# A retention layer with a gated feed-forward layer on one core: when two units' loads and transposes are issued

## Chip, cores and metric

One core of a Trainium2 chip. The metric is the device time of one execution in microseconds (us). Engine names in the profile: PE is the matrix engine (PEld its weight loads), DVE the vector engine, ACT the scalar engine, POOL is GpSimd, SP is SyncE, which here only issues transfers; a "q" behind a name is that engine's sequencer.

## The reference

A retention recurrence over 768 steps for 4 batches and 8 heads of 64, with one decay per head, then RMS normalisation and a SwiGLU layer over all 3072 tokens:

```
gamma = 1.0 - 2.0 ** (-5.0 - np.arange(H))
for t in range(S):
    state = gamma[None, :, None, None] * state + einsum('bhd,bhe->bhde', k[:, :, t], v[:, :, t])
    y[:, :, t] = scale * einsum('bhd,bhde->bhe', q[:, :, t], state)
x = y.transpose(0, 2, 1, 3).reshape(B * S, H * D)          # 3072 x 512
xn = x / sqrt(mean(x * x) + 1e-6) * rms_g
g = xn @ w_gate                                            # 512 x 1536
out = (g * sigmoid(g) * (xn @ w_val)) @ w_out              # 1536 x 512
```

Inputs and output are float32.

## The kernel before

The 768 steps are cut into six chunks of 128. A chunk has four **units**, one a batch, written (c, b); two units are a **pair** (c, p), and the j-th unit of a pair is (c, p, j). Chunks 0 and 1 use a paired layout of rows; chunks 2 to 5 use plain units.

A unit from chunk 2 on is worked as follows. `load(c, b)` (L105) issues three transfers on POOL's queue: q and k, cast to bf16, and v. `t_dma(c, b)` (L470) issues two transposing transfers on SP's queue, qb to qT and kb to kT. `vp` (L466) scales v by the decay on POOL. `a_pe` (L480) makes the scores on PE, `a_mask` (L489) masks them on DVE. `values(c, p)` (L504) makes for a pair y_ps (scores times v), kv_ps (the update of the state) and y_ps again (q times state); with `then` it makes a pair's scores (`a_pair`, two `a_pe`) at its end. Then come `y_out` (DVE), `state_add` (DVE), `square` (ACT), `rstd` (POOL: m at L454, the power at L370), `state_cast` (POOL, L348), `norm` (DVE, L462) and `x_dma(c, p, j)` (L541), a transposing transfer on SP that fills xnT, the feed-forward layer's input. x(2,1,1) below is such a transfer. In chunk 1 two further helpers, `tp1` and `tc1`, transpose q and k on PE and copy them out as q2T and k2T, `ap` makes the scores (L280), and `x_pe` and `x_copy` transpose xn on PE.

The feed-forward layer of a chunk is a row of `gv` steps (L548: eight g_ps and eight v_ps matmuls of 256 tokens, or four and four of 512, a sigmoid-weighted unit on ACT, a product on DVE into hT) and four `down(c, b)` (L576: twelve matmuls of hT with w_out into o_ps, a copy to o_sb on ACT, a store on SP; o_sb has three buffers). It lags one chunk behind: while PE runs the feed-forward steps of chunk c, the retention work of chunk c+1 and the loads of chunk c+2 are put between the steps.

The order is written out by hand. Every engine and every queue serves its instructions in program order. The first part of the program is a plain list of calls; from chunk 1's feed-forward on, `run(steps, after)` calls the steps and, behind step number i, whatever `after[i]` lists. One dictionary (L752) serves chunk 1's steps: 0 to 5 are `gv` of the first 256 tokens, 6 to 11 of the second, 12 to 15 the downs. Another (L785) serves chunks 2 to 5: steps 0 and 1 are `gv` of the first 256 tokens, 2 and 3 of the second, 4 to 11 `gv` of all 512, 12 to 15 the downs. d there is the chunk in its retention phase and d+1 the one being loaded.

PSUM has eight banks. `bank` hands them out in a fixed rotation up to chunk 1's feed-forward (`split`), and after that four for the feed-forward and four for the retention work.

Of the kernel before, what the change touches and what calls it, by code (L numbers as in the profile page):

```python
# [16 lines left out]
def kernel(  # L17
# [21 lines left out]
    NFF = DFF // 128  # L39
# [25 lines left out]
    def bank(name, dtype=F32, ffn=False, i=None):  # L65
        if i is None and split[0]:
            i = turn[ffn] % 4 + 4 * ffn
            turn[ffn] += 1
        elif i is None and first:
            i = first.pop(0)  # L70
        elif i is None:
            i = order[0]
            order.append(order.pop(0))
        return psum.tile([128, 512 if dtype == F32 else 1024], dtype, name=name, tag=f"p{i}")
# [30 lines left out]
    def load(c, b, names="qkv"):  # L105
        u = U.setdefault((c, b), {})
        for n in names:
            if n == "v":
                x = work.tile([128, H, D], F32, name="v_f", tag="v_f", bufs=6)
                nc.gpsimd.dma_start(out=x, in_=unit_v[n][c, b])  # L110
            else:
                x = work.tile([128, DM], BF16, name=n + "b", bufs=8)
                nc.gpsimd.dma_start(out=x.rearrange("p (h d) -> p h d", h=H), in_=unit_v[n][c, b])  # L113
            u[n] = x
# [106 lines left out]
    def copy(eng, out, in_):  # L221
        return (nc.scalar.copy if eng == "a" else nc.vector.tensor_copy)(out, in_)  # L222
# [44 lines left out]
    def ap(c, p, a):  # L267
        u = U[c, p]
        if c == 0:
            qt, kt = ([u[n + "T", a][:, :, b] for b in range(2)] for n in "qk")  # L270
        else:
            qt, kt = u["qT", a], u["kT", a]
        ps = [bank("a_ps") for _ in range(2)]
        for x in range(2):
            for e in range(2):
                o = (x * 2 + e) * 128
                for b in range(2):
                    for i in range(2):
                        r, t = slice(i * 64, i * 64 + 64), slice(b * 64, b * 64 + 64)
                        nc.tensor.matmul(ps[i][t, o:o + 128], kt[b][r, x, e], qt[b][r, x], start=True, stop=True)  # L280
        u["a_ps", a] = ps
# [104 lines left out]
    def x_pe(c, p, j):  # L386
        u = U[c, p]
        ps = bank("x_ps", BF16)
        for s in range(KS):
            nc.tensor.transpose(ps[:, s * 128:(s + 1) * 128], u["xn"][j][:, s * 128:(s + 1) * 128], ident)  # L390
        u["x_ps", j] = ps

    def x_copy(c, p, j, eng):
        b = 2 * p + j
        dst = XT[c][:, :, b * C:(b + 1) * C]
        src = U[c, p]["x_ps", j][:, :512].rearrange("p (s t) -> p s t", s=KS)
        if c == 0 and j == 0:
            nc.vector.tensor_tensor(out=dst, in0=src, in1=g_col[:, :, None].to_broadcast([128, KS, 128]), op=ALU.mult)
        else:
            return copy(eng, dst, src)  # L400
# [71 lines left out]
    def t_dma(c, b):  # L472
        u = U[c, b]
        for n in "qk":
            t = work.tile([128, NHP, 128], BF16, name=n + "T", tag=n + "T", bufs=8)
            nc.sync.dma_start_transpose(out=t, in_=u[n])
            u[n + "T"] = t
# [91 lines left out]
    def store(eng, c, b, m, o_sb):  # L569
        if c < 2:  # L570
            for e in range(2):
                eng.dma_start(out=out_e[c, b, e][:, m], in_=o_sb[e * 64:e * 64 + 64, m])
        else:
            eng.dma_start(out=out_v[c, b][:, m], in_=o_sb[:, m])

    def down(c, b):  # L576
        ps = bank("o_ps", ffn=True)
        for n in range(NFF):
            nc.tensor.matmul(ps, HT[c][:, n, b * C:(b + 1) * C], wo_b[:, n, :], start=n == 0, stop=n == NFF - 1)  # L579
        o_sb = work.tile([128, DM], F32, name="o_sb", bufs=3)  # L580
        nc.scalar.copy(o_sb, ps)  # L581
        store(nc.sync, c, b, slice(0, DM), o_sb)
# [125 lines left out]
    load(2, 0)  # L708
    y1(0)
    down(0, 0)  # L710
    y1_out(0)
    square(1, 0, 0)
# [5 lines left out]
    vp_pair(1, 1)  # L718
    load(2, 2)
    down(0, 1)  # L720
    down(0, 2)
    t_dma(2, 0)
    for n, e in (("q", "a"), ("k", "v")):
        tp1(1, n)
        tc1(1, n, e)
# [1 line left out]
    x_copy(1, 0, 0, "v")  # L727
    x_pe(1, 0, 1)
    x_copy(1, 0, 1, "v")
    ap(1, 1, 0)  # L730
    ap(1, 1, 1)
    for a in range(2):
# [1 line left out]
            ap_mask(1, 1, a, i)  # L734
    load(2, 3)
    t_dma(2, 1)
    down(0, 3)

    def run(steps, after):
        for i, step in enumerate(steps):  # L740
            step()
            for f in after.get(i, ()):
                f()

    def L(f, *a):
        return lambda: f(*a)
# [13 lines left out]
        5: [L(a_pair, 2, 0), L(a_mask, 2, 0, 0)],  # L760
        6: [L(a_mask, 2, 0, 1), L(a_mask, 2, 1, 0), L(vp, 2, 2), L(vp, 2, 3)],
        7: [L(a_mask, 2, 1, 1)],
        8: [L(values, 2, 0), L(y_out, 2, 0, 0), L(y_out, 2, 0, 1), L(state_add, 2, 0), L(load, 3, 2),
            L(t_dma, 3, 0), L(t_dma, 3, 1)],
        9: [L(square, 2, 0, 0), L(load, 3, 3)],
        10: [L(a_pair, 2, 1), L(square, 2, 0, 1), L(a_mask, 2, 2, 0), L(a_mask, 2, 2, 1), L(state_cast, 0),
             L(rstd, 2, 0)],
        11: [L(a_mask, 2, 3, 0), L(a_mask, 2, 3, 1), L(t_dma, 3, 2)],
        12: [L(values, 2, 1, (3, 0), True), L(norm, 2, 0, 0, 1), L(x_dma, 2, 0, 0), L(x_dma, 2, 0, 1),
             L(y_out, 2, 1, 0), L(y_out, 2, 1, 1), L(square, 2, 1, 0), L(square, 2, 1, 1), L(rstd, 2, 1),  # L770
             L(state_add, 2, 1), L(a_mask, 3, 0, 0), L(a_mask, 3, 0, 1), L(norm, 2, 1, 0, 1),
             L(x_dma, 2, 1, 0), L(x_dma, 2, 1, 1), L(t_dma, 3, 3), L(a_mask, 3, 1, 0, 1),
# [3 lines left out]
    for c in range(2, NCH):  # L776

        steps = [L(gv, c, n, n + 2, t, t + 256) for t in (0, 256) for n in (0, 2)]
        steps += [L(gv, c, n, n + 1, 0, GT) for n in range(4, NFF)]
        steps += [L(down_last if (c, b) == (NCH - 1, B - 1) else down, c, b) for b in range(B)]  # L780
        d = c + 1
        more = d + 1 < NCH
        after = {}
        if d < NCH:
            after = {  # L785
                0: [L(begin, d)] + [L(load, d + 1, 0)] * more,
                1: [L(values, d, 0)] + [L(load, d + 1, 1)] * more,
                2: [L(y_out, d, 0, 0), L(vp, d, 2), L(vp, d, 3)],
                3: [L(y_out, d, 0, 1)] + [L(state_add, d, 0)] * more,
                4: [L(square, d, 0, 0)] + [L(t_dma, d + 1, 0)] * more,  # L790
                5: [L(a_pair, d, 1), L(a_mask, d, 2, 0), L(square, d, 0, 1), L(rstd, d, 0)]
                   + [L(state_cast, 0), L(t_dma, d + 1, 1)] * more,
                6: [L(a_mask, d, 2, 1), L(norm, d, 0, 0), L(x_dma, d, 0, 0)] + [L(load, d + 1, 2)] * more,
                7: [L(norm, d, 0, 1), L(x_dma, d, 0, 1), L(a_mask, d, 3, 0)] + [L(vp, d + 1, 0)] * more,
                8: [L(a_mask, d, 3, 1)] + [L(load, d + 1, 3), L(vp, d + 1, 1)] * more,
            }
            if more:
                after.update({
                    11: [L(values, d, 1, (d + 1, 0), True), L(y_out, d, 1, 0), L(y_out, d, 1, 1),
                         L(square, d, 1, 0), L(square, d, 1, 1), L(rstd, d, 1), L(state_add, d, 1),  # L800
                         L(a_mask, d + 1, 0, 0), L(a_mask, d + 1, 0, 1), L(norm, d, 1, 0, 1), L(x_dma, d, 1, 0)],
                    12: [L(x_dma, d, 1, 1), L(a_mask, d + 1, 1, 0, 1), L(state_cast, 1), L(t_dma, d + 1, 2)],
                    13: [L(t_dma, d + 1, 3)],
                })
            else:
                after.update({
                    9: [L(values, d, 1)],
                    10: [L(y_out, d, 1, 0)],
                    11: [L(y_out, d, 1, 1), L(square, d, 1, 0), L(square, d, 1, 1), L(rstd, d, 1)],
                    12: [L(norm, d, 1, 0, 1), L(x_dma, d, 1, 0), L(x_dma, d, 1, 1)],  # L810
                })
        run(steps, after)
# [28 lines left out]
```

## Time and profile before

| | us |
|---|---|
| median of 4 runs | 239.37 (238.26, 238.68, 240.06, 242.51) |
| the profiled execution | 237.91 |
| its span, first to last instruction | 236.1 |
| PE busy in it | 225.9 |

The granted PE clock is full throughout. The busy tenths of PE and of the transfer engines over 40 equal slices of 5.9 us:

```
PE   7986999999999999998999999999999999999994
DMA  7999999999999999899993999992530204200022
```

In the list of issues the q and k loads of a unit take a median of 6.0 and 6.7 us from issue to landing, v 7.1; the transposes qT 6.4, kT 7.7 and xnT 4.2.

To read the views: a row of the timeline gives start, duration, engine, line, operation and tiles, the number of instructions merged into it, and in brackets the engine's idle time before it with what ended that. A row of the waits gives who waited for whom: total us, times, longest. A row of the chain gives start, duration, and what held the chain then. A queue's row gives packets, MB, and the packets' time as a share of 16 engines.

### The profile page before, as it was taken

Reading aid. Unit: us, or ns where it says so; the run is one execution under the profiler, and the core shown is the slowest. Engines: PE = TensorE matmul, PEld = TensorE weight load, DVE = VectorE, ACT = ScalarE, POOL = GpSimd, SP = SyncE. Lnnn points to the kernel's source line nnn. Section 1 sums busy time; section 2 is a strip of 40 time slices with the busy share of each in tenths; the row PEclk is TensorE's granted clock in tenths of the full one; section 3 lists DMA queues with packets and bytes.
Section 4 is the critical chain, followed back from the end, with each engine's and each line's share of the span. In section 5 each row is a group of like instructions: output and inputs, shape, how many; then the busy total and the mean of one; then the engine's idle time right before and its main releaser. Section 6 shows DMA issues by size and latency. Waiting matters only on the chain.

```text
span 236.1 us, 5540 instructions
## 1 busy us (share of the span) xinstructions
PE 225.9 (96%) x2268; PEld 138.6 (59%) x2290; DVE 127.4 (54%) x222; ACT 87.5 (37%) x176; POOL 114.9 (49%) x150
## 2 busy tenths in 40 slices
PE   7986999999999998999999999999999999999994
PEld 2445785545898864684454684454774544854443
DVE  3675743828396787346967046967155742244300
ACT  2865535242343433225323235332325241333211
POOL 8967699759689934952927703917001000000000
PEclk9999999999999999999999999999999999999999
DMA  7999999999999999899993999992530204200022
GB/s 99 162 191 204 180 166 181 198 200 227 155 147 196 157 156 210 89 212 194 106 122 25 177 165 214 112 113 70 136 109 0 47 0 144 81 0 0 0 92 90
DMA packets 83307, 30.25 MB, mean 128 GB/s; under 512 B 69521, under 2 KB 78993, under 8 KB 83282
## 3 DMA queue, kind: packets, MB, share of 16 engines
q0 software_dynamic: 51328, 16.52, 72.5%
q1 hardware_dynamic: 31280, 13.25, 29.2%
q8 instruction: 18, 0.29, 0.5%
q10 hardware_dynamic: 674, 0.14, 0.3%
q14 instruction: 7, 0.06, 0.1%
HBM read 28.32 MB, written 6.29 MB: 147 GB/s over the span
## 4 chain that ended last, share of the span: by engine, by line
PE 83%; DMA 8%; POOL 4%; DVE 2%; issue 1%; ACT 1%; POOLq 0%; DVEq 0%
PE v_ps L560 25%; PE g_ps L560 24%; PE o_ps L579 24%; DMA wv_b<-in_moe_w_val_dram 4%; DMA kT<-kb 4%; PE a_ps L485 1%; PE y_ps L514 1%; POOL q2b L101 1%; POOL k2b L101 1%; PE o_ps L590 1%; PE y_ps L531 1%; PE kv_ps L523 1%; POOL wg_b L86 1%; PE kv_ps L329 1%; DVE x L440 1%
## 5 line engine op out<-in xcount | busy, mean ns | idle before, releaser
L565 DVE TENSOR_TENSOR hT<-sg,v_ps 128x512 bf16<-128x512 bf16 (+1 forms) x76 | 49.9, 658 | 76.0 <-PE v_ps L560 64.6
L560 PE MATMUL v_ps<-xnT,wv_b 128*128 128x256 bf16 (+1 forms) x427 | 74.9, 309 | 1.9 <-DMA wv_b<-in_moe_w_val_dram 1.6
L560 PE MATMUL g_ps<-xnT,wg_b 128*128 128x256 bf16 (+1 forms) x417 | 73.8, 308 | 0.8 <-ACT xnT L222 0.2
L564 ACT ACTIVATE sg<-g_ps 128x512 bf16<-128x512 f32 (+1 forms) x76 | 43.5, 575 | 74.8 <-PE g_ps L560 70.5
L579 PE MATMUL o_ps<-wo_b,hT 128*128 128x512 bf16 x269 | 60.6, 379 | 0.4
L560 PEld LDWEIGHTS <-wv_b 128*128 128x128 bf16 x428 | 41.7, 98 | 22.8 <-DMA wv_b<-in_moe_w_val_dram 2.2
L560 PEld LDWEIGHTS <-wg_b 128*128 128x128 bf16 x428 | 40.5, 98 | 21.1 <-issue 0.7
L579 PEld LDWEIGHTS <-hT 128*128 128x128 bf16 x276 | 26.6, 98 | 31.6
L454 POOL TENSOR_SCALAR m<-ms 128x2 f32<-128x2 f32 x10 | 2.2, 218 | 69.7 <-ACT xsq L449 69.6
L581 ACT COPY o_sb<-o_ps 128x512 f32<-128x512 f32 x23 | 13.5, 585 | 46.1 <-PE o_ps L579 42.5
L462 DVE SCALAR_TENSOR_TENSOR xn<-x,rstd,g_bc 128x512 bf16<-128x512 f32 x20 | 19.5, 1005 | 9.3 <-POOL rstd L370 9.3
L494 DVE TENSOR_TENSOR am<-a_ps,causal 128x512 bf16<-128x512 f32 x32 | 21.1, 681 | 0.0
L468 POOL TENSOR_TENSOR vp<-v_f,vd_n 128x512 bf16<-128x512 f32 x16 | 19.4, 1236 | 0.0
L449 ACT ACTIVATE xsq<-x 128x512 bf16<-128x512 f32 x20 | 12.4, 623 | 9.3 <-DVE x L440 9.3
L113 POOL DMA_DIRECT2D kb<-in_k_dram x16 | 14.4, 898 | 1.9 <-DMA wo_b<-in_moe_w_out_dram 1.9
L113 POOL DMA_DIRECT2D qb<-in_q_dram x16 | 15.1, 943 | 0.0
L110 POOL DMA_DIRECT2D v_f<-in_v_dram x16 | 14.7, 921 | 0.0
L440 DVE TENSOR_TENSOR x<-y_ps,yd_n 128x512 f32<-128x512 f32 x16 | 10.6, 685 | 1.7 <-PE y_ps L531 1.7
L219 PE MATMUL hot<-ones 128*128 128x512 bf16 x25 | 9.6, 503 | 1.5 <-DVE ones L146 1.4
L300 POOL TENSOR_TENSOR vp<-v2f,vd_p 128x1024 bf16<-128x1024 f32 x4 | 7.7, 1928 | 0.4 <-DMA v2f<-in_v_dram 0.4
L370 POOL TENSOR_TENSOR rstd<-m,mhalf 128x2 f32<-128x2 f32 x10 | 7.2, 718 | 0.8
L101 POOL DMA_DIRECT2D q2b<-in_q_dram x8 | 5.8, 736 | 0.8 <-POOLq L825 0.8
(96 smaller groups left out, 154.7 us busy)
## 6 DMA issues: line engine op xcount, KB each, us to landing
v_f<-in_v_dram POOLq DMA_DIRECT2D x16, 256.0 KB, 7.1
out_dram<-o_sb SPq DMA_DIRECT2D x15, 256.0 KB, 2.3
out_dram<-o_sb SPq DMA_DIRECT2D x17, 128.0 KB, 5.5
qb<-in_q_dram POOLq DMA_DIRECT2D x16, 128.0 KB, 6.0
kb<-in_k_dram POOLq DMA_DIRECT2D x16, 128.0 KB, 6.7
wg_b<-in_moe_w_gate_dram POOLq DMA_DIRECT2D x6, 256.0 KB, 7.9
wv_b<-in_moe_w_val_dram POOLq DMA_DIRECT2D x6, 256.0 KB, 8.6
wo_b<-in_moe_w_out_dram POOLq DMA_DIRECT2D x3, 512.0 KB, 8.9
```

What stands on the lines that cost most here:

```text
L110: nc.gpsimd.dma_start(out=x, in_=unit_v[n][c, b])
L113: nc.gpsimd.dma_start(out=x.rearrange("p (h d) -> p h d", h=H), in_=unit_v[n][c, b])
L440: nc.vector.tensor_tensor(out=x[:, :, :, i, :], in0=u["y"][i].rearrange("p (b a d) -> p b a d", b=2, a=NHP), in1=yd_n[:, c, i][:, None, :, ...
L449: nc.scalar.activation(xsq, u["x"][:, b], AF.Square, scale=1.0 / math.sqrt(DM), accum_out=u["ms_"][:, b:b + 1])
L462: nc.vector.scalar_tensor_tensor(out=u["xn"][b], in0=u["x"][:, b], scalar=u["rstd"][:, b:b + 1], in1=g_bc, op0=ALU.mult, op1=ALU.mult)
L468: nc.gpsimd.tensor_tensor(out=x, in0=U[c, b]["v"], in1=vd_n[:, c, :, None].to_broadcast([128, H, D]), op=ALU.mult)
L494: nc.vector.tensor_tensor(out=x, in0=u["a_ps"][i].rearrange("p (a t) -> p a t", a=NHP), in1=causal[:, None, :].to_broadcast([128, NHP, 128 ...
L560: nc.tensor.matmul(x[:, o:o + w], wt[:, s, n * 128:(n + 1) * 128], XT[c][:, s, t0:t1], start=s == 0, stop=s == KS - 1)
L564: nc.scalar.activation(sg[:, :m], ps[0][:, :m], AF.Silu)
L565: return nc.vector.tensor_tensor(out=HT[c][:, n0:n1, t0:t1], in0=sg[:, :m].rearrange("p (n t) -> p n t", t=w), in1=ps[1][:, :m].rearrange( ...
L579: nc.tensor.matmul(ps, HT[c][:, n, b * C:(b + 1) * C], wo_b[:, n, :], start=n == 0, stop=n == NFF - 1)
L581: nc.scalar.copy(o_sb, ps)
```

## The change

`down` can be given a part of its twelve matmuls: n0 to n1 into the same bank, with copy and store behind the last part alone. Otherwise instructions only change places:

- Chunk 0's feed-forward: the two transposes of unit (2,0) go before `down(0, 2)` instead of behind it; `down(0, 3)` is cut into four matmuls ahead of `ap(1, 1, 0)` and eight at its old place.
- Chunk 1's steps: `load(3, 2)` from step 8 to 11, `load(3, 3)` from step 9 to 12; the transposes of (3,2) from step 11 into step 12, between the x transposes of the pairs (2,0) and (2,1). Those of (3,3) stay behind the latter.
- Chunks 2 and 3 (d+1 is 4 and 5): `load(d+1, 0)` and `load(d+1, 1)` from steps 0 and 1 to 1 and 3, the transposes of these units from steps 4 and 5 to 5 and 6, and `load(d+1, 2)` to the head of step 6's list.

```diff
-    def down(c, b):
-        ps = bank("o_ps", ffn=True)
-        for n in range(NFF):
+    DP = {}
+
+    def down(c, b, n0=0, n1=NFF):
+        ps = DP[b] = bank("o_ps", ffn=True) if n0 == 0 else DP[b]
+        for n in range(n0, n1):
             nc.tensor.matmul(ps, HT[c][:, n, b * C:(b + 1) * C], wo_b[:, n, :], start=n == 0, stop=n == NFF - 1)
+        if n1 < NFF:
+            return
...
     down(0, 1)
+    t_dma(2, 0)
     down(0, 2)
-    t_dma(2, 0)
...
     x_copy(1, 0, 1, "v")
+    down(0, 3, 0, 4)
     ap(1, 1, 0)
     ap(1, 1, 1)
...
     t_dma(2, 1)
-    down(0, 3)
+    down(0, 3, 4)
...
-        8: [L(values, 2, 0), L(y_out, 2, 0, 0), L(y_out, 2, 0, 1), L(state_add, 2, 0), L(load, 3, 2),
+        8: [L(values, 2, 0), L(y_out, 2, 0, 0), L(y_out, 2, 0, 1), L(state_add, 2, 0),
             L(t_dma, 3, 0), L(t_dma, 3, 1)],
-        9: [L(square, 2, 0, 0), L(load, 3, 3)],
+        9: [L(square, 2, 0, 0)],
...
-        11: [L(a_mask, 2, 3, 0), L(a_mask, 2, 3, 1), L(t_dma, 3, 2)],
+        11: [L(a_mask, 2, 3, 0), L(a_mask, 2, 3, 1), L(load, 3, 2)],
         12: [L(values, 2, 1, (3, 0), True), L(norm, 2, 0, 0, 1), L(x_dma, 2, 0, 0), L(x_dma, 2, 0, 1),
+             L(t_dma, 3, 2), L(load, 3, 3),
...
-                0: [L(begin, d)] + [L(load, d + 1, 0)] * more,
-                1: [L(values, d, 0)] + [L(load, d + 1, 1)] * more,
+                0: [L(begin, d)],
+                1: [L(values, d, 0)] + [L(load, d + 1, 0)] * more,
                 2: [L(y_out, d, 0, 0), L(vp, d, 2), L(vp, d, 3)],
-                3: [L(y_out, d, 0, 1)] + [L(state_add, d, 0)] * more,
-                4: [L(square, d, 0, 0)] + [L(t_dma, d + 1, 0)] * more,
+                3: [L(y_out, d, 0, 1)] + [L(state_add, d, 0), L(load, d + 1, 1)] * more,
+                4: [L(square, d, 0, 0)],
                 5: [L(a_pair, d, 1), L(a_mask, d, 2, 0), L(square, d, 0, 1), L(rstd, d, 0)]
-                   + [L(state_cast, 0), L(t_dma, d + 1, 1)] * more,
-                6: [L(a_mask, d, 2, 1), L(norm, d, 0, 0), L(x_dma, d, 0, 0)] + [L(load, d + 1, 2)] * more,
+                   + [L(state_cast, 0), L(t_dma, d + 1, 0)] * more,
+                6: [L(t_dma, d + 1, 1), L(load, d + 1, 2)] * more + [L(a_mask, d, 2, 1), L(norm, d, 0, 0), L(x_dma, d, 0, 0)],
```

## The prediction

> **What bounds the kernel now.** I began with the busy shares on the page, then the matrix engine's own waits from 40 us on, then its timeline around the two it shows, then the chain of waits into the longer one, and last the two queues that feed that chain.
>
> ```profile
> PE 225.9 (96%) x2268; PEld 138.6 (59%) x2290; DVE 127.4 (54%) x222; ACT 87.5 (37%) x176; POOL 114.9 (49%) x150
> ```
>
> ```profile
> PE a_ps L485 <- DMA kT<-kb: 0.8, 1, 0.8
> PE a_ps L280 <- ACT q2T L222: 0.2, 1, 0.2
> ```
>
> PE is busy for 225.9 of 236.1 us, and from 40 us on it waits over 0.15 us only twice. Both waits lie in code that the diff touches. The change adds and removes no arithmetic, so what it can gain is these two waits; what it can lose is any new one.
>
> ```profile
> 55.97 0.24 PE L280 MATMUL a_ps<-q2T,k2T 64*64 64x128 bf16 x2
> 56.41 0.63 PE L280 MATMUL a_ps<-q2T,k2T 64*64 64x128 bf16 x30 [0.19 <-ACT q2T L222]
> ...
> 88.85 0.39 PE L485 MATMUL a_ps<-qT,kT 64*128 64x128 bf16 x8
> 90.06 0.40 PE L485 MATMUL a_ps<-qT,kT 64*128 64x128 bf16 x8 [0.82 <-DMA kT<-kb]
> ```
>
> ```profile
> 81.27 8.75 DMA kT<-kb
> 90.01 0.05 issue
> 90.06 0.40 PE a_ps L485 x8
> ```
>
> The first stall is at `ap(1,1,0)`: PE has the scores' first operand but not the second q2T copy. The second is at `a_pe(3,1)`: its k transpose was issued at 81.27 and landed 8.75 us later. What stood beside that transfer is in the GpSimd and SyncE timelines:
>
> ```profile
> 77.60 0.94 POOL L113 DMA_DIRECT2D qb<-in_q_dram  x1
> 78.52 0.91 POOL L113 DMA_DIRECT2D kb<-in_k_dram  x1
> 79.38 0.93 POOL L110 DMA_DIRECT2D v_f<-in_v_dram  x1
> 80.26 0.93 POOL L113 DMA_DIRECT2D qb<-in_q_dram  x1
> 81.12 0.94 POOL L113 DMA_DIRECT2D kb<-in_k_dram  x1
> 81.99 0.96 POOL L110 DMA_DIRECT2D v_f<-in_v_dram  x1
> ```
>
> ```profile
> 85.01 1.19 SPq L476 DMA_TRANSPOSE qT<-qb  x1
> 86.30 2.09 SPq L476 DMA_TRANSPOSE kT<-kb  x1
> 88.49 1.19 SPq L572 DMA_DIRECT2D out_dram<-o_sb  x2
> 89.77 7.71 SPq L543 DMA_TRANSPOSE xnT<-xn  x4
> ```
>
> The six loads of units (3,2) and (3,3) are issued from 77.60 to 82.95, exactly around the transposes of (3,1) at 79.77 and 81.27. Transposes with little beside them land fast: 2.4 us at the least (x transposes, after 160 us).
>
> **Part 1: the split down and t_dma(2,0).** Four of the twelve matmuls of `down(0,3)` come before `ap(1,1,0)`. In the timeline the twelve run at a pitch of 0.216 us, so four fill 55.97 to 56.84. The awaited q2T copy ended at 56.35, the k2T copies at 56.25: the thirty-two score matmuls then run unbroken. Before, the third of them started at 56.41 although the first two started at 55.97: 0.43 us lost, of which the page calls 0.19 idle (the rest is the pipeline's tail). The split costs one more switch of matmul shapes; the nearest rows are groups after a switch, 0.98 against 0.87 us for the same eight matmuls at 62.88: 0.11. Bounds of the cost: 0 and 0.22 (two switches); I take 0.1. Gain 0.33. The bank order moves with it, o_ps(0,3) taking the bank that a_ps had, and each a_ps the next one: the new owners of the score banks are the copies of `down(0,2)` (ended at 55.38) and of q2T and k2T (56.35), all before 56.84. The first bank of the next stage, for g_ps at about 59.2, was read by the second mask, which ended at 58.11 before and ends about 0.5 later: no wait.
>
> Of `t_dma(2,0)` two transposes pass two stores of `down(0,2)` on SP. They were issued at 56.61 and 58.10 and can go when kb(2,0) is there (landed at 54.93), so SP is free of `t_dma(2,1)` about 2.2 us sooner; that waits for kb(2,1) at 59.34 and so is issued at 59.7 rather than 61.91. Its k took 9.5 us and landed at 71.4, needed at 72.09: a cover of 0.7 us that PE's gain would eat, and that grows to about 2.5. The stores go 2 us later; their o_sb is wanted again at 93.19. Gain of the move itself: nothing.
>
> **Part 2: loads and transposes of (3,2), (3,3).** On POOL the order becomes cast of the state, m, rstd(2,0), then the six loads. The cast waits for the state add (ended at 81.16), m for the last square (83.27, now 0.3 sooner), rstd takes 0.72: the loads run from about 83.9 to 89.4 instead of 77.6 to 82.95. Behind them on POOL stands rstd(2,1), whose square ended at 91.77 and will end near 90.4: a cover of 1.0 us. If it were gone, norm(2,1) and its transposes would slip by the same amount.
>
> So (3,1)'s transposes have no newly issued load beside them from 77.6 on, only the tail of those issued until 75.6 (landed at 82.7). kT(3,1) lands at 81.27 plus 2.4 to 7.5 (the k of (3,0) before it took 7.0, q 7.5), thus 83.7 to 88.8; I take 86. PE asks at 89.07 less 0.33: even the upper bound arrives in time. The weight loads of that line waited 1.0 us and the matmuls started 0.99 us late (last start before 89.02, next 90.06, pitch 0.05). Gain 0.99, of which 0.82 is idle.
>
> What comes next: on SP the order becomes stores of `down(1,0)`, x(2,0,0), x(2,0,1), q and k of (3,2), x(2,1,0), x(2,1,1), then (3,3). With stores at 88.2 and each transpose taking 1.2 to 1.3 us to issue: x(2,0) from 89.5 to 92.1, (3,2) to 94.6 (its q is loaded from 83.9 and lands between 5.3 and 10.2 us later by the rows of that tile, 89.2 to 94.1; nearest is 5.3, of the load that met the emptiest queues), x(2,1,0) to 95.9, x(2,1,1) issued at 95.9. Before, that last one was issued at 95.45 and took 4.4 us. Landing at 100.3. PE wants it at 102.94 less the 1.3 gained, 101.6. No wait, with 1.3 us to spare. (3,3) is issued at the same 97.6 as before, and wanted at 110. Cost taken: 0.
>
> **Part 3: chunk 4, and chunk 5 the same way.** The vp products of the running chunk (2.10 us for two) pass before the second unit's loads on POOL; on SP nothing changes order from `t_dma(4,0)` on. Loads of (4,1), issued from 99.00, move by 2.1 less 1.3: 0.8 later. kT(4,1) is issued at 108.92, wanted at 122.25. For chunk 5: issue at 129.37, scores at 157.09. Cost 0 both times, covered by some ten us. One place is tight already: the last x transpose of chunk 3, issued at 129.20, took 8.3 us and landed at 137.5, wanted at 137.77. It moves with PE, and the loads of (5,1) issued beside it at 129.37 now come 2.1 us after: if anything it gets room.
>
> [...] Transposes without loads beside them took 4.1 and 4.4 us (x(2,1)); with loads beside them 5.0 and 8.3 us (x(3,1)). In the stretch from 86 to 89 us the two queues moved the same number of packets:
>
> ```profile
> q1 hardware_dynamic: 885, 0.22, 96.0%
> q0 software_dynamic: 881, 0.11, 80.5%
> ```
>
> [...]
>
> By the rows, what decides is x(2,1,1). At 8.3 us it would land at 104.2, 2.6 us late, and the sum would be +1.3. At 4.4 it is -1.3. The moved loads are issued by 89.4, 6.5 us before it, and beside it are only three loads of (4,0), as there are now; I take 4.4 and keep 8.3 for the range.
>
> **Sum.** 0.33 + 0.99 = 1.32, about 1.3 us. The profiled execution took 237.91 us (span 236.1 and 1.8 around it), so 236.6. That execution lies 0.35 under the lowest of the four runs and 1.46 under their median, 239.37, which a run of 242.51 widens: the changed kernel's median then lies between 236.95 and 238.05. I say 237.9, nearer to the median's own offset.
>
> **Rivals.**
> - *It turns slower*: x(2,1,1) lands late behind (3,2)'s two transposes and the loads. For: SP serves strictly in order, 2.5 us of issue are put ahead of it, and 8.3 us is measured for its twin. Against: SP was idle for norm(2,1) just there, so its issue moves by 0.45 us only. It costs from a latency of 5.7 us on, and makes the kernel slower than before from 7.0 on; at 8.3 it is +1.3, thus 240.7.
> - *The long stall stays*: the transposes of (3,1) were slow by what was ahead of them (loads until 75.6 and (3,0)'s transposes), not by what came after. For: v(3,1) itself landed 8 us after its issue at 74.70. Against: packets of the two queues go one for one, so later loads do take part. Then only 0.33 is gained: 239.0.
> - *Both go, but a cover is lost*: rstd(2,1) or kT of another unit gives back about half: -0.65, 238.7.
>
> **How the numbers follow.** Forecast 0.66; slower 0.10; stall stays 0.10; half given back 0.14. The forecast's own range, 236.6 to 238.6, comes from the offset to the median and the 0.22 of the split. Taking in the second and third rival up to some scatter of the median (the two middle runs are 1.4 apart) gives 236.5 to 239.6. One per cent, about what a measurement of this kernel tells from no change, is 2.4 us: faster means under 237.0, which only the lower end of the forecast reaches: 0.15. Slower means over 241.8, beyond 8.3 us of latency or an ill-placed run: 0.07. Within: 0.78.
>
> **What would show it.** Right: PE's wait for kT at `a_pe(3,1)` is gone and kT lands within 7.5 us; no q2T wait; the six loads start at about 84; PE waits nowhere else after 40 us; span near 234.8. Wrong: a gap at the first g_ps of the second token half of chunk 2, about 101.6, released by xnT; a gap at `a_pe(3,1)` as before; or rstd(2,1) late behind the loads on POOL.

## The result and the profile after

| | before | after |
|---|---|---|
| median, us | 238.62 (236.37 to 248.37, 65 executions) | 241.88 (237.68 to 247.08, 41 executions) |
| the profiled execution, us | 237.91 | 241.88 |
| its span, us | 236.1 | 240.1 |
| its mean granted PE clock | 1.000 | 0.992 |

The ratio of the times is 1.0057, with a 95% interval of 1.0035 to 1.008: the changed kernel is slower by about half a per cent. The ratio compares the executions within 1.5% of each kernel's fastest; most of the changed kernel's, the profiled one among them, lie above that, so its median is 1.4% up. The forecast was 237.9 in a range up to 239.6, with the sign the other way.

The 41 executions fall into two groups: 29 have a mean granted clock of 0.995 or less and a median of 243.66, 12 a higher clock and a median of 239.5. The profiled one is of the first group. Its busy shares, then PE's waits from 47 us on (who waited for whom; total us, times, longest):

```profile
PE 226.2 (94%) x2268; PEld 138.9 (58%) x2290; DVE 129.7 (54%) x222; ACT 87.5 (36%) x176; POOL 115.0 (48%) x150
```

```profile
PE a_ps L485 <- DMA kT<-kb: 1.8, 1, 1.8
PE g_ps L560 <- DMA xnT<-xn: 0.4, 1, 0.4
PE x_ps L390 <- DVE xn L462: 0.4, 1, 0.4
```

Both waits of before are gone: none on the q2T copy and none at `a_pe(3,1)`. There are three others, and the first row looks like the old one without being it. PE's timeline shows which unit it is:

```profile
58.10 0.64 PE L280 MATMUL a_ps<-q2T,k2T 64*64 64x128 bf16 x32
...
83.61 0.40 PE L485 MATMUL a_ps<-qT,kT 64*128 64x128 bf16 x8
85.84 0.42 PE L485 MATMUL a_ps<-qT,kT 64*128 64x128 bf16 x8 [1.84 <-DMA kT<-kb]
86.19 1.89 PE L560 MATMUL g_ps<-xnT,wg_b 128*128 128x256 bf16 x8
87.88 1.83 PE L560 MATMUL v_ps<-xnT,wv_b 128*128 128x256 bf16 x8
93.31 0.61 PE L485 MATMUL a_ps<-qT,kT 64*128 64x128 bf16 x16
...
106.92 1.05 PE L560 MATMUL g_ps<-xnT,wg_b 128*128 128x256 bf16 x8 [0.44 <-DMA xnT<-xn]
```

The first line is `ap(1,1,0)`, unbroken as forecast. 93.31 is the scores of (3,0) and (3,1), sixteen matmuls in one piece: the wait that the change was to remove is gone. But 85.84 is `a_pe(2,3)`, eight microseconds earlier in the program, which waited for nothing before (the sixteen matmuls of (2,2) and (2,3) ran in one piece there):

```profile
82.77 0.62 PE L485 MATMUL a_ps<-qT,kT 64*128 64x128 bf16 x16
```

And 106.92 is the second token half of chunk 2, x(2,1,1)'s reader. After the first wait, groups of eight that take 1.04 take 1.89 and 1.83. The table by stretches (length, busy us and instructions of PE, PEld, DVE, ACT, POOL, then the granted clock, transfer share, GB/s) tells why:

```profile
82.00:88.00 6.00, 4.16 (x41) 3.03 (x39) 2.58 (x4) 1.50 (x5) 4.33 (x7) 0.84 1.35 140
88.00:94.00 6.00, 5.95 (x85) 3.90 (x85) 3.69 (x6) 1.19 (x2) 2.57 (x3) 0.88 1.50 162
```

The granted clock is 0.84 and 0.88: the records hold one stretch of 3.41 us at half clock, from 86.09 on. The wait of 1.84 is thus paid nearly twice, since 3.41 us at half clock do 1.71 us of work less. The chain of waits names what both new waits stand behind:

```profile
75.42 10.38 DMA kT<-kb
85.80 0.05 issue
85.84 0.42 PE a_ps L485 x8
...
101.75 5.12 DMA xnT<-xn
106.87 0.05 issue
106.92 1.05 PE g_ps L560 x8
```

A ledger by stages follows from the starts of PE's first matmul of each (the first o_ps, the first y_ps of chunk 1's second pair, then in each `values` the second y_ps, q times state), in us:

| stage on PE | before | after | difference |
|---|---|---|---|
| start to first o_ps | 46.81 | 47.62 | +0.81 |
| first o_ps to the y_ps of chunk 1's second pair | 14.51 | 14.54 | +0.03 |
| to `values(2,0)` | 17.51 | 17.52 | 0 |
| to `values(2,1)`, holds `a_pe(2,3)` | 9.77 | 13.40 | +3.63 |
| to `values(3,0)`, holds `a_pe(3,1)` | 13.99 | 12.99 | -1.00 |
| to the next, holds x(2,1,1)'s reader | 19.25 | 19.76 | +0.51 |
| all later stages | 114.29 | 114.28 | 0 |

The 0.81 before the first o_ps is code that is the same in both kernels; that start lies between 46.1 and 49.2 us in the kernels below. What the change did is in the rest, 189.32 against 192.49: 1.00 won, 3.63 and 0.51 lost. The stage from the first o_ps on holds a loss of its own (the norm at 54.46 took 2.39 us on DVE and held x_ps up by 0.35), which hides the split's gain.

### The profile page after: what moved, and what is told of

It reads as the page before. It is cut to its first block, busy times and chain, and to the rows that moved or that the text cites. A ratio compares the mean times of both kernels' runs of the same rounds, so it can differ in the third digit from the quotient of the medians.

```text
span 240.1 us, 5536 instructions
## 1 busy us (share of the span) xinstructions
PE 226.2 (94%) x2268; PEld 138.9 (58%) x2290; DVE 129.7 (54%) x222; ACT 87.5 (36%) x176; POOL 115.0 (48%) x150
## 4 chain that ended last, share of the span: by engine, by line
PE 75%; DMA 11%; DVE 5%; POOL 5%; issue 1%; ACT 1%; SPq 0%; POOLq 0%; DVEq 0%
PE v_ps L560 24%; PE g_ps L560 23%; PE o_ps L581 19%; DMA wv_b<-in_moe_w_val_dram 5%; DMA kT<-kb 4%; DVE xn L462 2%; DMA xnT<-xn 2%; PE a_ps L485 1%; POOL q2b L101 1%; PE y_ps L514 1%; POOL k2b L101 1%; PE o_ps L594 1%; DVE am L494 1%; PE y_ps L531 1%; PE kv_ps L523 1%
## 5 line engine op out<-in xcount | busy, mean ns | idle before, releaser
L560 PE MATMUL v_ps<-xnT,wv_b 128*128 128x256 bf16 (+1 forms) x427 | 75.7, 312 | 2.0 <-DMA wv_b<-in_moe_w_val_dram 1.7
L560 PE MATMUL g_ps<-xnT,wg_b 128*128 128x256 bf16 (+1 forms) x417 | 74.7, 311 | 1.9 <-DMA wg_b<-in_moe_w_gate_dram 0.8
L462 DVE SCALAR_TENSOR_TENSOR xn<-x,rstd,g_bc 128x512 bf16<-128x512 f32 x20 | 21.9, 1122 | 9.3 <-POOL rstd L370 9.3
L440 DVE TENSOR_TENSOR x<-y_ps,yd_n 128x512 f32<-128x512 f32 x16 | 10.6, 685 | 1.7 <-PE y_ps L531 1.7
L219 PE MATMUL hot<-ones 128*128 128x512 bf16 x25 | 8.4, 446 | 1.6 <-DVE ones L146 1.4
L485 PE MATMUL a_ps<-qT,kT 64*128 64x128 bf16 x128 | 5.1, 217 | 1.8 <-DMA kT<-kb 1.8
```

The costliest lines, as they stand in the source:

```text
L440: nc.vector.tensor_tensor(out=x[:, :, :, i, :], in0=u["y"][i].rearrange("p (b a d) -> p b a d", b=2, a=NHP), in1=yd_n[:, c, i][:, None, :, ...
L462: nc.vector.scalar_tensor_tensor(out=u["xn"][b], in0=u["x"][:, b], scalar=u["rstd"][:, b:b + 1], in1=g_bc, op0=ALU.mult, op1=ALU.mult)
L560: nc.tensor.matmul(x[:, o:o + w], wt[:, s, n * 128:(n + 1) * 128], XT[c][:, s, t0:t1], start=s == 0, stop=s == KS - 1)
```

## The experiments

Two theories stood after that reading. **A**: the early `t_dma(2,0)` slows the loads of (2,2) and (2,3), and through them kT(2,3). **B**: the transposes of (3,2) between those of the two pairs make x(2,1,1) late. **C**, the rival, said that the moves in chunks 4 and 5 cost something. Below, "rest" is the time from the first o_ps matmul to the end in that kernel's profile, "halved" the number of its executions with a mean granted clock of 0.995 or less, wherever in the kernel the clock fell: in the profiles of e4 and e9 the one such stretch starts at 22.73 and 23.32 us, ahead of everything that the change moves. Ratios are against the kernel before on the same chip.

### Each part alone

The changed kernel with `t_dma(2,0)` back at its old place (e1); the kernel before with that move alone (e2), with the loads and transposes of (3,2) and (3,3) alone (e3), with the split alone (e4), and with the moves of chunks 4 and 5 alone (e5). Here are the edits of e1 (against after), and of e2 (against before); e3, e4 and e5 take their hunks from the diff of the change as they are.

```diff
     down(0, 1)
-    t_dma(2, 0)
     down(0, 2)
+    t_dma(2, 0)
```

```diff
-    down(0, 2)
     t_dma(2, 0)
+    down(0, 2)
```

```diff
-        8: [L(values, 2, 0), L(y_out, 2, 0, 0), L(y_out, 2, 0, 1), L(state_add, 2, 0), L(load, 3, 2),
+        8: [L(values, 2, 0), L(y_out, 2, 0, 0), L(y_out, 2, 0, 1), L(state_add, 2, 0),
...
+             L(t_dma, 3, 2), L(load, 3, 3),
```

```diff
+    down(0, 3, 0, 4)
     ap(1, 1, 0)
...
-    down(0, 3)
+    down(0, 3, 4)
```

```diff
-                0: [L(begin, d)] + [L(load, d + 1, 0)] * more,
+                0: [L(begin, d)],
...
-                   + [L(state_cast, 0), L(t_dma, d + 1, 1)] * more,
+                   + [L(state_cast, 0), L(t_dma, d + 1, 0)] * more,
```

> The changed kernel with one part undone: the two transposes of unit (2,0) stand behind down(0,2) again. Theory A (the early transposes of chunk 2 push the loads of (2,2) and (2,3) back, so that the k transpose of (2,3) lands after the scores a_pe(2,3) ask for it, PE stops there and the granted clock halves for 3.4 us behind it): the wait of 1.84 us at a_pe(2,3) is gone, kb(2,3) lands 11 us after its issue and not 13.25, the granted clock of the span is 0.997 or more in most executions, and the ratio to before is 0.993 to 0.997, the forecast gain. Theory B (the x transposes of pair (2,1), put behind the transposes of (3,2), are late for chunk 2's second token half): the wait of 0.44 us on xnT stays or grows, ratio 1.000 to 1.006. Theory C (the loads of chunks 4 and 5): ratio above 1.003 with waits behind 110 us.

> The kernel before with one part of the change alone: the two transposes of unit (2,0) ahead of down(0,2). Theory A: slower, ratio 1.005 to 1.015, a wait of 1 to 2 us at a_pe(2,3) on kT, a halved clock behind it in about half of the executions, kb(2,3) landing 12 to 13 us after its issue where it was 10.9. Theories B and C: ratio 0.998 to 1.002, no such wait. My forecast, which set this move at nothing, says the same as B and C.

> The kernel before with the moves of (3,2) and (3,3) alone (their loads three steps later, the transposes of (3,2) between the x transposes of the two pairs of chunk 2). Theory A: the wait of 0.82 us at a_pe(3,1) is gone and nothing takes its place, ratio 0.994 to 0.998. Theory B: that wait is gone and one of 0.5 to 2.5 us on xnT at chunk 2's second token half has come, ratio 1.000 to 1.008. Theory C: as A.

> The kernel before with the split of down(0,3) alone: four of its twelve matmuls ahead of the scores of pair (1,1). All theories: the wait of 0.19 us on q2T is gone, PE gains 0.3 us, ratio 0.997 to 1.001. If the moved bank of o_ps matters, a wait shows at the first g_ps of chunk 1 and the ratio is above 1.001.

> The kernel before with the moves of chunks 4 and 5 alone. Theory C: ratio above 1.002 and a wait behind 110 us. Theories A, B and D: nothing; ratio 0.997 to 1.002, the stretches of PE behind values(3,0) 15.58, 19.25, 15.21 and 15.43 us as before.

| | median | ratio | halved | rest | waits of PE in its profile |
|---|---|---|---|---|---|
| e1 | 239.35 | 1.0046 [1.0001, 1.009] | 5 of 12 | 195.90 | `a_pe(2,3)` 4.14, xnT 0.27 |
| e2 | 241.43 | 1.0017 [0.998, 1.0054] | 8 of 12 | 195.44 | `a_pe(2,3)` 2.60, `a_pe(3,1)` 1.75 |
| e3 | 239.96 | 1.0033 [0.9991, 1.0074] | 6 of 12 | 193.13 | xnT 2.44 |
| e4 | 238.8 | 1.0023 [0.9988, 1.0059] | 8 of 12 | 189.62 | `a_pe(3,1)` 1.14 |
| e5 | 238.94 | 1.0012 [0.9982, 1.0043] | 4 of 12 | 188.69 | none over 0.4 |

The kernel before had medians of 238.47 (e1 to e4; 12 of 35 halved) and 238.14 (e5; 12 of 36) beside them. C falls: the moves in chunks 4 and 5 show no wait and the same stages behind `values(3,0)` as before. e5 has no wait at `a_pe(3,1)` although its loads of (3,2) and (3,3) are where they were, so that wait too comes in some executions and not in others. e4 shows the wait on the q2T copy gone, but no gain in time: its wait at `a_pe(3,1)` is 0.32 longer than before's, and its ratio, 1.0023, lies above the 1.001 that was forecast. e3 shows B in its purest form:

```profile
PE g_ps L560 <- DMA xnT<-xn: 2.4, 1, 2.4
```

e2 shows A's wait with nothing else changed; the ratio of 1.005 to 1.015 that A forecast for it did not come, since 1.0017 is not told from 1. And A in its strict form, that putting `t_dma(2,0)` back removes the wait, missed: e1's profile has the longest one so far.

```profile
PE a_ps L485 <- DMA kT<-kb: 4.1, 1, 4.1
PE v_ps L560 <- ACT o_sb L585: 0.4, 1, 0.4
PE g_ps L560 <- DMA xnT<-xn: 0.3, 1, 0.3
```

That execution took 244.19, where e1's median is 239.35. So one profile did not settle it: the wait comes in some executions and not in others, and what had to be compared was how often.

### Taking each wait's reader or its rival away

Two edits answer A and B each. *x first*: the transposes of (3,2) go behind those of pair (2,1). *Late scores*: `a_pe(2,3)` goes one step later, which gives kT(2,3) some 1.95 us more (2.18 between the starts of the scores of (2,2) and (2,3) in e8, for 0.23 before). e7 is the changed kernel with x first, e8 with late scores, e9 with both; e10 is the kernel before with late scores.

```diff
-             L(t_dma, 3, 2), L(load, 3, 3),
+             L(load, 3, 3),
...
-             L(x_dma, 2, 1, 0), L(x_dma, 2, 1, 1), L(t_dma, 3, 3), L(a_mask, 3, 1, 0, 1),
+             L(x_dma, 2, 1, 0), L(x_dma, 2, 1, 1), L(t_dma, 3, 2), L(t_dma, 3, 3), L(a_mask, 3, 1, 0, 1),
```

```diff
-        10: [L(a_pair, 2, 1), L(square, 2, 0, 1), L(a_mask, 2, 2, 0), L(a_mask, 2, 2, 1), L(state_cast, 0),
+        10: [L(a_pe, 2, 2), L(square, 2, 0, 1), L(a_mask, 2, 2, 0), L(a_mask, 2, 2, 1), L(state_cast, 0),
...
-        11: [L(a_mask, 2, 3, 0), L(a_mask, 2, 3, 1), L(load, 3, 2)],
+        11: [L(a_pe, 2, 3), L(a_mask, 2, 3, 0), L(a_mask, 2, 3, 1), L(load, 3, 2)],
```

> The changed kernel with the transposes of (3,2) behind the x transposes of pair (2,1) instead of between the pairs; the late loads stay. Theory B, as the first four runs shaped it (every profile with the moves of chunk 3 has a wait on xnT at chunk 2's second token half, 0.44, 0.27 and 2.4 us, none without them has): the wait on xnT is gone, x(2,1,1) lands 2 us or more before it is asked for; ratio 0.4 to 1.0 per cent below the changed kernel's 1.0057. Theory D (the k transpose of (2,3) is late for a_pe(2,3) in many executions, because chunk 2's transfers are spread widely from execution to execution, and each such wait of over 1.8 us is followed by 3.4 us at half the granted clock): a_pe(2,3) can still wait, so half of the executions still show a clock of 0.993 or less. If neither wait matters the ratio stays at 1.004 to 1.008.

> The changed kernel with the scores of (2,3) one step later (behind the last gv of chunk 1 instead of the one before it), so that the k transpose has 1.9 us more. Theory D: the waits at a_pe(2,3) are gone or shorter by 1.9 us, executions with a granted clock of 0.995 or less fall from 71 in 100 to under 45, the median of all executions falls by 1 us or more against the changed kernel's 241.9. Theory B: the wait on xnT stays and the ratio of the fast runs stays near 1.005.

> Both edits on the changed kernel: x transposes of pair (2,1) ahead of those of (3,2), and the scores of (2,3) one step later. If B and D together are the cause, this is what I had forecast for the change: ratio of the fast runs 0.993 to 0.998, executions with a clock of 0.995 or less under 35 in 100, no wait over 0.5 us on PE behind 50 us. If something else is the cause: ratio over 1.002.

> The kernel before with the scores of (2,3) one step later alone. Theory D: the slow tail of the kernel before (12 of 35 executions with a clock of 0.995 or less) comes in part from the same wait, so it thins to under 25 in 100, and the fast runs stay within 0.3 per cent of before. If a_pe(2,3) is only late in the changed kernel: no difference in either.

| | median | ratio | halved | rest | waits of PE in its profile |
|---|---|---|---|---|---|
| e7 | 239.84 | 0.9989 [0.9933, 1.0045] | 3 of 12 | 194.46 | `a_pe(2,3)` 4.07 |
| e8 | 241.47 | 1.004 [0.9986, 1.0094] | 8 of 12 | 192.07 | xnT 1.91 |
| e9 | 239.15 | 0.9968 [0.9932, 1.0004] | 6 of 12 | 188.94 | none over 0.5 |
| e10 | 239.48 | 1.0053 [1.0013, 1.0094] | 4 of 12 | 189.91 | `a_pe(3,1)` 0.85 |

The kernel before had 238.92 beside them (16 of 35 halved). Each edit takes away its own wait and leaves the other, and both together leave none, which speaks for two separate causes. e9's profile is weak support for late scores, though: its kT(2,3) landed at 83.08 and would have been in time for the old place too, at 85.5. In e8 it landed 1.3 us too late for the old place and in time for the new one. Late scores are not free either: the stage to `values(2,1)` takes 9.99 with them and 9.77 without. e8 and e9 missed their forecasts of under 45 and under 35 halved in 100. e10 is a miss that stays open: its profile has 0.22 for the late scores and a wait of 0.35 on x_ps that before's lacks, but its ratio, 1.0053, stands for 1.3 us.

### The two suspects on one chip

e12 is the changed kernel with both suspects undone (the edits of e1 and e7 together), e16 repeats e7 (only the early `t_dma(2,0)` left as suspect), e17 repeats e1 (only the order of (3,2) left), e15 is the changed kernel itself.

> The changed kernel with both suspects undone: the transposes of (2,0) behind down(0,2), those of (3,2) behind the x transposes of pair (2,1). All else of the change stays: the split, the late loads, chunks 4 and 5. If the two suspects carry the loss: ratio of the fast runs 0.993 to 0.999, executions with a clock of 0.995 or less under 30 in 100, first o_ps to the end 187.8 to 188.3 us, no wait on PE over 0.5 us behind 50 us. If something else of the change loses: ratio over 1.002.

> The changed kernel itself, the corner with both suspects in it, beside the other three on one chip: ratio 1.003 to 1.008 as it was measured, two of three executions with a halved clock, a wait on xnT in its profile, and the slowest median of the four.

> The corner of the square with the early transposes of (2,0) alone left as a suspect (the transposes of (3,2) behind the x transposes), beside its neighbours on one chip. If the early transposes push chunk 2's last loads back: v(2,3) lands 12 us or more after its issue (9 to 11 in the corner with both undone), kT(2,3) lands within 2 us of the time at which a_pe(2,3) asks for it or behind it, more executions with a halved clock than with both undone.

> The corner with the order of (3,2) before the x transposes of pair (2,1) alone left as a suspect. If that order costs: a wait on xnT of 0.2 to 2.5 us at chunk 2's second token half, the stretch from values(2,1) to values(3,0) 19.5 to 23.5 us and not 19.25, ratio 0.3 to 0.8 per cent above the corner with both undone; kT(2,3) lands 3 us or more before it is asked for.

| | early `t_dma(2,0)` | (3,2) between | median | ratio | halved | rest |
|---|---|---|---|---|---|---|
| e12 | no | no | 238.08 | 1.001 [0.9968, 1.0051] | 1 of 12 | 187.83 |
| e17 | no | yes | 239.37 | 1.0025 [0.998, 1.007] | 5 of 12 | 191.69 |
| e16 | yes | no | 244.13 | 1.0158 [1.007, 1.0246] | 6 of 6 | 196.30 |
| e15 | yes | yes | 240.82 | 0.9998 [0.9932, 1.0065] | 6 of 12 | 191.25 |

The kernel before had 238.61 here (9 of 29 halved). By medians each suspect costs something and neither leaves e12's time, but the intervals of e12, e17 and e15 overlap, and that e16 (six executions) lies above e15, which has both, shows how far such a set scatters. Three forecasts missed here: e12's of a ratio under 0.999, e17's of 0.3 to 0.8% above e12, and e15's of 1.003 or more and the slowest median. The profiles are clearer. e15's has both waits, 1.22 at `a_pe(2,3)` and 1.37 on xnT, and ran at full clock: its rest is 1.93 above before's, from +0.10, +1.39, -1.00 and +1.44 in the four stages of the ledger that moved. That is nearer to the 1.4 us for which the ratio of 1.0057 stands than the 3.17 of the halved execution. e12 has no wait on PE after 47 us. **B** is seen beside it in e17's waits, and in the two queues (SP, then POOL) of e17, of e12 and of before:

```profile
PE g_ps L560 <- DMA xnT<-xn: 2.1, 1, 2.1
```

```profile
91.82 1.21 SPq L476 DMA_TRANSPOSE qT<-qb  x1
93.12 1.22 SPq L476 DMA_TRANSPOSE kT<-kb  x1
94.43 3.54 SPq L543 DMA_TRANSPOSE xnT<-xn  x2
```

```profile
95.30 0.99 POOL L113 DMA_DIRECT2D qb<-in_q_dram  x1
```

```profile
89.92 6.97 SPq L543 DMA_TRANSPOSE xnT<-xn  x4
96.99 2.05 SPq L476 DMA_TRANSPOSE qT<-qb  x1
```

```profile
96.52 0.99 POOL L113 DMA_DIRECT2D qb<-in_q_dram  x1
```

```profile
94.00 3.48 SPq L543 DMA_TRANSPOSE xnT<-xn  x2
```

```profile
96.27 0.99 POOL L113 DMA_DIRECT2D qb<-in_q_dram  x1
```

The transfer that e17's chain waits for, then the landing of the same one in e12:

```profile
95.75 7.34 DMA xnT<-xn
103.10 0.04 issue
103.14 0.90 PE g_ps L560 x4
```

```profile
DMA to landing us min/median/max: 4.0/4.0/4.0
```

In e17 the second of the two x transposes, x(2,1,1), is issued at 95.75, behind (3,2)'s two, and 0.45 after q(4,0)'s load. It took 7.34 us and landed at 103.10; PE had been free since 101.02. In e12 it is issued at 95.69, 0.83 ahead of that load, and took 3.99. This holds throughout: in the six profiles with (3,2) between the pairs the load is issued 0.45 to 1.48 us ahead of x(2,1,1), which takes 5.0 to 7.3 us, and all six have a wait on it (0.27 to 2.44). In the twelve others the load comes behind it, or at most 0.06 ahead; it takes 2.5 to 4.6 us, and none has the wait. That the load ahead of it is what stretches the transfer was not tried by itself: in all six the two transposes of (3,2) also go just ahead of it, and they are a rival that no run separates from the load.

**A** shows in e16's waits and in PE's timeline:

```profile
PE a_ps L485 <- DMA kT<-kb: 5.6, 2, 4.3
```

```profile
88.50 0.61 PE L485 MATMUL a_ps<-qT,kT 64*128 64x128 bf16 x8 [4.27 <-DMA kT<-kb]
```

Two waits: 1.29 at the scores of (2,1), 4.27 at `a_pe(2,3)`; the clock was halved for 6.83 us from 87.08 on, inside the second wait. The stretch from 58 to 61 us, while the loads of chunk 2's last two units run, in e16 and then in e12 (columns as above):

```profile
58.00:61.00 3.00, 3.00 (x25) 2.13 (x23) 1.81 (x4) 1.18 (x2) 3.00 (x4) 1.00 1.49 92
```

```profile
58.00:61.00 3.00, 3.00 (x31) 1.88 (x20) 2.44 (x4) 0.71 (x2) 3.00 (x4) 1.00 2.76 240
```

92 GB/s against 240 over all queues; the eight profiles with the early transposes have 92 to 158, the ten without 189 to 251. More than half of that gap lies in SP's queue and not in the loads: SP's queue, where the move puts two stores behind the transposes, moved 0.10 MB in e16 and 0.37 in e12, POOL's queue 0.16 and 0.33. Over 58 to 64 us the packets' time on POOL's queue fills a share of 71% to 125% with the early transposes and of 143% to 242% without, and no profile lies in between. But the bytes don't part that way; here are before and after:

```profile
q0 software_dynamic: 1942, 0.46, 170.4%
```

```profile
q0 software_dynamic: 1944, 0.50, 107.4%
```

Nearly as many packets, and no fewer bytes. How the early transposes hold the loads up therefore stays open; that the loads land later shows in their landings. v(2,3), issue to landing, in e16 and in e12:

```profile
DMA to landing us min/median/max: 15.2/15.2/15.2
```

```profile
DMA to landing us min/median/max: 10.1/10.1/10.1
```

Over all profiles it is 11.8 to 15.2 us (mean 13.6, eight of them) with the early transposes, and 9.1 to 14.0 (mean 10.6, ten) without. kT(2,3) can only be issued when its load is there. It landed late for the old place of `a_pe(2,3)`, by 1.3 to 4.4 us, in six of the eight, and in one of the ten; that one is e1. So the early transposes make the wait common, they aren't the only thing that can make it. The clock counts agree: of all executions 70 of 119 are halved with the early transposes and 35 of 108 without, where the kernel before, run beside the experiments, has 49 of 135.

### A better version

e11 is the kernel before with the early `t_dma(2,0)` and late scores: does room for kT(2,3) make that move worth anything? e13 is the kernel before with the late loads of (3,2) and (3,3) and x first. e14 joins what had shown a gain or cover: the changed kernel with `t_dma(2,0)` back, x first and late scores.

```diff
-    t_dma(2, 0)
     down(0, 2)
+    t_dma(2, 0)
...
+        10: [L(a_pe, 2, 2), L(square, 2, 0, 1), L(a_mask, 2, 2, 0), L(a_mask, 2, 2, 1), L(state_cast, 0),
...
+             L(x_dma, 2, 1, 0), L(x_dma, 2, 1, 1), L(t_dma, 3, 2), L(t_dma, 3, 3), L(a_mask, 3, 1, 0, 1),
```

> The kernel before with the early transposes of (2,0) and the scores of (2,3) one step later. Theory A and D together (the early transposes push the k transpose of (2,3) back, and that costs only through the wait at a_pe(2,3)): the executions with a clock of 0.995 or less fall from the 67 in 100 of the early transposes alone to about 40, kT(2,3) lands after the old time of a_pe(2,3) but before the new one, or at most 1 us behind it. If the early transposes cost through something else, about 67 in 100 stay.

> The kernel before with the late loads of (3,2) and (3,3) alone, and the transposes of (3,2) behind the x transposes of pair (2,1). Theory B: both the wait at a_pe(3,1) and the wait on xnT are gone, the stretch of PE from values(2,1) to values(3,0) is 19.25 us as before and the one ahead of it 12.99 instead of 13.99; ratio of the fast runs 0.994 to 0.999, below the 1.0033 that the same loads gave with the transposes of (3,2) between the pairs. If the late loads cost something in another way: over 1.000.

> What the runs so far leave over as gains, together: the split of down(0,3), the late loads of (3,2) and (3,3) with their transposes behind the x transposes, the moves of chunks 4 and 5, the scores of (2,3) one step later, and the transposes of (2,0) at their old place. Theories B and D: no wait on PE over 0.5 us behind 50 us, the time from the first o_ps matmul to the end 188.6 to 189.1 us (189.3 before), executions with a clock of 0.995 or less under 35 in 100, ratio 0.993 to 0.998. If the early transposes of (2,0) are harmless (theory A wrong altogether): no better than the same kernel with them, which had 0.9968.

| | median | ratio | halved | rest | waits of PE in its profile |
|---|---|---|---|---|---|
| e11 | 239.67 | 1.001 [0.9976, 1.0043] | 4 of 12 | 192.13 | `a_pe(3,1)` 2.24, kv_ps 0.58 |
| e13 | 238.12 | 1.0016 [0.9987, 1.0044] | 0 of 12 | 188.97 | 0.47 at the scores of (3,2), q2T 0.19 |
| e14 | 237.18 | 0.9975 [0.9938, 1.0011] | 2 of 12 | 188.04 | none |

The kernel before had 238.14 beside them (12 of 36 halved). e14 has the lowest median of all and a rest 1.28 us under before's, but its interval takes in no change, and its rest lies 0.21 above that of e12, which leaves out the late scores. e11's profile does not answer its question: kT(2,3) landed 2 us ahead even of the old place of `a_pe(2,3)`. e13 shows what the late loads do when x goes first: no wait at `a_pe(3,1)`, none on xnT, and not one halved execution; but its ratio, forecast at 0.994 to 0.999, is 1.0016, and whether the late loads cost something in another way stays undecided. The halving is rare in e12, e13 and e14 (1, 0 and 2 of 12); e9, whose profile has neither wait, has 6 of 12, so the count doesn't follow these two waits alone.

## Why the prediction was wrong

**What held.** *Gain 0.33* of the split: with nothing else in the way (e1, e8, e12, e14, e16, e17) the stage from the first o_ps on is 14.01 against 14.51, so 0.50. *Gain 0.99* of the late loads: the stage to `values(3,0)` is 12.99 against 13.99, 1.00, in every profile that has them (of the six others five wait there, e5 alone doesn't). kT(3,1) landed 3.3 us after its issue in e12, inside 2.4 to 7.5. The six loads start at 84.58 there (83.9 forecast), end at 89.97, and rstd(2,1) behind them starts at 92.39: that cover held. Part 3, *cost 0*, held in e5. The *sum*, -1.32, is the rest of e12 to two tenths: 187.83 less 189.32 is -1.49. The rival in which the long stall stays fell.

**The step that failed first: "Gain of the move itself: nothing"**, of `t_dma(2,0)`. I followed what waits for the moved transposes, (2,0) and (2,1), and what they pass, and never asked which transfers would then run beside them. These are the loads of (2,2) and (2,3), issued from 58.6 to 63.9 us in the changed kernel. The cover that mattered was kT(2,3)'s, some 3 us in the profile of before, and no number in the prediction stood for it. Even the gain in cover that I did forecast for kT(2,1), to 2.5 us, did not come: it was to be issued at 59.7, and was issued at 62.29 in the changed kernel, no sooner than the 61.91 of before, since kb(2,1) took 6.67 us to land and not 5.25. In e16 the scores of (2,1) waited 1.29 us. In the profile of after this step is worth 3.63, more than the 3.17 that the time from the first o_ps to the end lost on balance. That the move makes such waits common is what the runs show; how it slows the loads is open.

**The step that failed second: x(2,1,1), "I take 4.4"**, with its reason, *"beside it are only three loads of (4,0), as there are now"*. The issue was near what was forecast: 95.75 in e17 for 95.9, 5.27 us ahead of its reader for 5.7. The latency was mis-sized, 5.0 to 7.3 us for 4.4. The reason overlooked an order: before, the transpose went 0.8 us ahead of the first of these loads; with 1.3 us won by PE and two transposes put ahead of it on SP it came behind that load. The prediction also counts the 4.4 among transposes without loads beside them, though q(4,0) was issued 0.82 us into it. Whether the load or the two transposes stretch it, no run separates. The rival that turns slower named both, with 5.7 us as the point from which a wait begins, and got a tenth. In the profile of after 5.12 us sufficed, since the transpose was issued at 101.75 and PE was there at 106.48, 4.73 later. That packets of the two queues go one for one, as the second rival has it, is the row of one stretch (885 on SP's queue to 881 on POOL's, 86 to 89 us); from 89 to 95 us the same profile has 2392 to 1205.

**What no term stood for: the clock.** Every wait was priced at its length. A wait of 1.84 us cost 3.63 where the clock halved behind it. With it the account of e17 closes: -1.49 + 2.12 of wait + 1.71 for 3.41 us at half clock is +2.34, measured 191.69 less 189.32, +2.37.

**The time as a whole.** The forecast of "within 1%" named a start of 0.35 to 1.46 us off the median; the part before the first o_ps alone scatters by 3 us. So even e12, which does what was forecast, can't be told from before by its times: 1.001 with an interval of 0.9968 to 1.0051.

## What to carry to other kernels

When a transfer is moved earlier, look at the transfers that it will now run beside, and at the cover of *their* readers, not only at its own; here the order alone did not tell how long a transfer took (v(2,3): 9.1 to 14.0 us in ten profiles that order it alike). Where PE waits in one execution and not in the next, count over many executions, and price what follows a wait with it: in five of six profiles with a wait of 1.84 to 2.60 us, 3.41 us at half clock followed, and in the profile of after the stage with the wait of 1.84 took 3.63 more. In a kernel that is 96% busy the last microsecond is lost sooner by a new wait than it is won by removing an old one: undo a change part by part and keep those whose stage got shorter.

## What was not expected of the hardware

A PE wait of 1.84 to 2.60 us was mostly followed by a stretch of 3.41 us at half the granted clock (after, e2, e3, e8, e17), one of 4.1 to 4.3 by 3.41 or 6.83 us (e7; e1, e16). After the start-up, waits of 0.82 to 1.75 drew none, nor did one of 2.24 in e11. Why that one did not, and from which length on a wait does, stays open: no run varied the length of a wait by itself. In after's trace the two stretches at half clock start at 86.09 and 239.69 us, 45 times 3.413 us apart, in that of e3 at 12.84 and 105.00 us, 27 times. What sets that step no run shows. The start-up has such stretches too: e4's starts at 22.73, behind waits of 0.94 and 0.98.

The same transfer at the same place in the program took very different times from profile to profile: v(2,3) 9.1 to 14.0 us in ten profiles that order it alike. Why the norm of chunk 1 took about 2.4 us rather than 0.74 on DVE in five of the profiles, holding x_ps up by 0.35 to 0.43, stays open.
